# Attention beside a gated linear unit: K, Q and the output rows as dense tiles of 128 rows

## The chip, the cores and the metric

The kernel runs on one core of one Trainium2 chip. The metric is the device time of one execution in microseconds, the median of several runs. The core has a matrix engine (TensorE, PE in the profile; its weight loads are listed apart as PEld), a vector engine (VectorE, DVE), an engine for activation functions (ScalarE, ACT), a general engine (GpSimd, POOL), and SyncE (SP), which here only issues DMA transfers. Each runs its own list of instructions in order and waits on semaphores for the others. SBUF is the on-chip memory, of 128 partitions; PSUM holds matmul results in banks of 128 partitions by 512 numbers of 32 bits.

## What is computed

With x of 2048 rows and 640 columns, 32 heads of 20 columns, and a feed-forward width of 1728:

```python
xn = layernorm(x)                                # no scale, no shift
q, k, v = split(xn @ wqkv)                       # 32 heads of 20 columns each
p = softmax(q @ k.T / sqrt(20))                  # per head, 2048 x 2048
s = concat_heads(p @ v) @ wo
h = sigmoid(xn @ w_gate) * (xn @ w_up)
g = silu(h @ w_down)
out = x + s * g
```

Inputs and the output are bf16.

## The kernel before

**Tiles.** The work on attention is cut into passes: 4 chunks of 512 queries, and in each 8 groups of 4 heads, so 32 passes. A pass has 16 tiles of 128 keys for 4 heads, that is 64 score banks of 128 keys by 512 queries, and the whole program has 2048 of them. A head has only 20 columns, so the kernel lays each of the four heads of a group into a band of 32 partitions: `kT_all` holds K transposed, bands of 32 partitions by group by 2048 keys, and a tile `qT` holds the group's queries in the same bands. In a band the first row is an extra one: 1 in K and in Q a bound on the scores, which is subtracted inside the score matmul; rows 1 to 20 are the head; the others are zero. The bound of a query is a matmul of the absolute values of q with the maxima of |k| (`k_max` L121, `k_most` L118, `k_bound` L115, `q_abs` L127).

**One score bank.** A score matmul (L879) writes a bank of PSUM. Banks are taken in sets of 3 and of 2 in turn, and ACT takes the exponential of a whole set in one instruction (L901). Now and then one more bank, called spare, is scored and its exponential is made by four operations on DVE (L912, L917, L921, L925), when the planner finds DVE's backlog short. Then PV matmuls (L999) add eight banks at a time into one PSUM bank, `oacc`, in which each head has a band: a row of the sum of the exponentials and 20 rows of output.

**End of a pass.** `normalise` (L660 to L697) copies `oacc` to SBUF (`oev`, L667), sends the sums of the exponentials out to DRAM and back on POOL's DMAs, takes reciprocals, broadcasts them back over the bands (`rl`, four DMAs, L684) and multiplies (`oT`, L696).

**The other work** fills gaps between scores on PE as "jobs", generators that emit a few matmuls at a time and then hand an eviction to DVE or ACT: `k_job` (L470, K of one group and 512 keys), `v_job`, `q_job` (L493, Q of one pass), `gateup_job` (L524), `down_job` (L564), `out_job` (L604, eight matmuls per half of 320 columns, one for each group, with the output weights in bands, `wo_pad`), and `part_job` (L631), which for the last query chunk multiplies the six groups that are done early. Jobs share two PSUM banks (`take_bank`, `give_bank`), and at most two are under way.

**What sets the order.** No engine chooses its order at run time: a planner in the Python program keeps a clock for PE, models of ACT and DVE with the cells that their operations wait for, and a due score bank for every job. K's job for a group is due 40 banks before the pass that needs it, Q's 24. A cell (`Cell`) holds the time at which the planner believes a result is there; a transfer counts 3.4 us. When nothing else is ready and PE would be idle for long, `zero_add` (L979 to L986) issues a matmul of zeros into `oacc`. SP takes its DMAs strictly in the order in which they are emitted, and its DMAs use eight semaphores in turn, so that each one waits until the eighth before it has landed.

**Setup and tail.** A setup stage normalises x, transposes it, makes K for the first group and Q for the first pass; the weights of K and Q are copied to bands by POOL (`wkp`, `wqp`, `pad_copy` L206), those of the output by 32 DMAs (`load_wo`, L754). After the last score, PE finishes the last partial products (L646), DVE copies the last `oacc` (L1080), and the last two groups are projected (L1088).

Of the kernel before, what the change touches and what calls it, by code (L numbers as in the profile page):

```python
# [14 lines left out]
P = 128  # L15
# [6 lines left out]
V_CHUNKS = ((0, 16), (16, 32))  # L22
OBUFS, WB = 1, 2
# [16 lines left out]
def kernel(  # L40
# [46 lines left out]
    mk_all = const.tile([P, NG, 4], FP32, name="mk_all")  # L87
    mk = const.tile([P, NG], FP32, name="mk")
    bound = const.tile([P, NG, P], BF16, name="bound")
# [7 lines left out]
    wqp = persist.tile([P, KD, HEAD, 32], BF16, name="wqp")  # L97
    wo_pad = persist.tile([P, NG, D], BF16, name="wo_pad")
# [4 lines left out]
    wkp = ep.tile([P, KD, HEAD, 32], BF16, name="wkp")  # L103
    wv = ep.tile([P, KD, D], BF16, name="wv")

    def k_matmuls(ps, g, cols):
        for kd in range(KD):
            nc.tensor.matmul(ps, lhsT=wkp[:, kd, GH * g:GH * g + GH, :].rearrange("p h e -> p (h e)"),  # L108
                             rhs=xnT[:, kd, cols],
                             start=(kd == 0), stop=(kd == KD - 1))  # L110
            yield

    def k_bound(g):
        k_most(g)
        nc.vector.tensor_scalar(out=bound[:, g, :], in0=esum, scalar1=mk[:, g:g + 1], scalar2=None, op0=ALU.mult)  # L115

    def k_most(g):
        nc.vector.tensor_reduce(out=mk[:, g:g + 1], in_=mk_all[:, g, :], axis=AXISX, op=ALU.max)  # L118

    def k_max(src, g, c):  # L120
        nc.vector.tensor_reduce(out=mk_all[:, g, c:c + 1], in_=src, axis=AXISX, op=ALU.max,  # L121
                                apply_absolute_value=True)

    def q_abs(ps):
        absq = wk.tile([P, QC], BF16, tag="absq", bufs=1, name="absq")
        high = ps.bitcast(U16).rearrange("p (q two) -> p q two", two=2)[:, :, 1]
        nc.vector.tensor_scalar(out=absq.bitcast(U16), in0=high, scalar1=0x7FFF, scalar2=None,  # L127
                                op0=ALU.bitwise_and)
        return absq
# [11 lines left out]
    def q_matmuls(ps, cols, g):  # L141
        for kd in range(KD):
            nc.tensor.matmul(ps, lhsT=wqp[:, kd, GH * g:GH * g + GH, :].rearrange("p h e -> p (h e)"),  # L143
                             rhs=xnT[:, kd, cols],
                             start=(kd == 0), stop=(kd == KD - 1))
            yield

    V_SETUP = 4
    qTs = {}
    with tc.tile_pool(name="setup", bufs=1) as sp, \
            tc.tile_pool(name="ps0", bufs=1, space=bass.MemoryType.PSUM) as ps0:
        x_sb = sp.tile([P, TT, D], BF16, name="x_sb")
        wk_raw = sp.tile([P, KD, D], BF16, name="wk_raw")
        wq_raw = sp.tile([P, KD, D], BF16, name="wq_raw")
# [20 lines left out]
        load_w(wk_raw, 1)  # L178
        load_x(12, 4)
        load_w(wq_raw, 0)  # L180
# [7 lines left out]
        nc.vector.memset(wkp[:, :, GH:HEAD, 1 + Dh:32], 0.0)  # L188
        for w in (wkp, wqp):
            nc.gpsimd.memset(w[:, :, 0:GH, 0:1], 0.0)  # L190
            nc.gpsimd.memset(w[:, :, 0:GH, 1 + Dh:32], 0.0)
# [13 lines left out]
        def pad_copy(dst, raw, g0, g1):  # L205
            nc.gpsimd.tensor_copy(  # L206
                out=dst[:, :, GH * g0:GH * g1, 1:1 + Dh],
                in_=raw[:, :, GH * g0 * Dh:GH * g1 * Dh].rearrange("p k (h e) -> p k h e", e=Dh))
# [38 lines left out]
        def k_mm(c):  # L247
            kps[c] = ps0.tile([P, 512], FP32, tag="k", bufs=KBUFS, name="ps_k")
            for _ in k_matmuls(kps[c], 0, slice(c * 512, (c + 1) * 512)):
                pass  # L250
# [16 lines left out]
        def q_mm():  # L267
            first["ps"] = ps0.tile([P, 512], FP32, tag="q", bufs=1, name="ps_q")
            for _ in q_matmuls(first["ps"], slice(0, QC), 0):
                pass  # L270

        def q_bound():
            nc.tensor.matmul(first["ps"], lhsT=bound[:, 0, :], rhs=first["abs"], start=False, stop=True,
                             skip_group_check=True)

        def q_evict():
            qT = wk.tile([P, QC], BF16, tag="qT", bufs=2, name="qT")
# [20 lines left out]
        op(("wkp",), "POOL", 0.52, ["wk"], lambda: pad_copy(wkp, wk_raw, 0, 1))  # L298
        ends["wk"], ends["wq"], ends["wv"] = 10.8, 14.7, 16.7
        op(("wqp",), "POOL", 0.52, ["wq"], lambda: pad_copy(wqp, wq_raw, 0, 1))  # L300
        for c in range(4):
            op(("k", c), "PE", 1.3, [("xnT", 4 * c + i) for i in range(4)] + [("wkp",)]
               + ([("kmax", c - KBUFS), ("kadd", c - KBUFS)] if c >= KBUFS else []), lambda c=c: k_mm(c), 0.2)
            op(("kmax", c), "DVE", 0.64, [("k", c)], lambda c=c: k_max(kps[c], 0, c))
            op(("kadd", c), "ACT", 0.57, [("kmax", c)], lambda c=c: k_add(c), 0.6 * (c == 3))
        op(("kmost",), "DVE", 0.2, [("kmax", c) for c in range(4)], lambda: k_most(0))
        op(("kbound",), "ACT", 0.3, [("kmost",)],
           lambda: nc.scalar.activation(out=bound[:, 0, :], in_=esum, func=ACT.Identity, scale=mk[:, 0:1]))
# [30 lines left out]

        nc.gpsimd.memset(wkp[:, :, GH:HEAD, 0:1], 0.0)  # L340
        pad_copy(wkp, wk_raw, 1, 2)
        nc.gpsimd.memset(wqp[:, :, GH:HEAD, 0:1], 0.0)
        nc.gpsimd.memset(wqp[:, :, GH:HEAD, 1 + Dh:32], 0.0)
        pad_copy(wqp, wq_raw, 1, 2)
        pad_copy(wkp, wk_raw, 2, NG)
        pad_copy(wqp, wq_raw, 2, NG)
        nc.gpsimd.memset(v_all[:, :, HH:HEAD, 0:1], 1.0)
        nc.gpsimd.memset(wo_pad.rearrange("p g d -> p (g d)"), 0.0)
# [113 lines left out]
    kb_cells = {0: Cell(0.0)}  # L462
# [7 lines left out]
    def k_job(g, c):  # L470
        cols = slice(c * 512, (c + 1) * 512)
        held, ps = yield "bank",
        for _ in k_matmuls(ps, g, cols):
            yield "mm", MM5
        k_cells[g, c] = dve.add(630.0, [Cell(pe[0] + PE_OUT)], lambda: nc.vector.tensor_scalar(
            out=kT_all[:, g, cols], in0=ps, scalar1=e0[:, 0:1], scalar2=None, op0=ALU.add), 1)
        give_bank(held, k_cells[g, c])
        most = dve.add(620.0, [k_cells[g, c]], lambda: k_max(kT_all[:, g, cols], g, c), 2)
        kb_cells.setdefault((g, "max"), []).append(most)
# [672 lines left out]
```

## Time and profile before

| | |
|---|---|
| median of 3 runs | 915.73 us (915.34 to 917.61) |
| the profiled execution | 916.7 us, its span 914.8 us |
| PE busy | 805.1 us, 88% |
| DVE busy | 837.8 us, 92% |
| ACT busy | 880.2 us, 96% |
| POOL busy | 167.7 us, 18% |
| DMA traffic | 49.5 MB, 54 GB/s over the span |

The first exponential of the main stage starts at 32.4 us and the last one ends at 896.6 us, so that a score bank takes 0.42 us on average.

A profile line of a group reads: line of the program, engine, operation, the tile written and the tiles read, shape and type, count; then the busy time in total and the mean of one in ns; then how long the engine stood idle in front of these instructions, and which instruction on which engine ended the wait. Times of neighbouring instructions overlap, so the distance from one start to the next can be shorter than the mean. A line by window gives its length, the busy time of PE, PEld, DVE, ACT and POOL with the number of instructions, the granted clock of PE (1.00 is full), the share of the DMA engines' time, and GB/s.

### The profile page before, as it was taken

How to read it: one execution, taken by the hardware profiler on the slowest of the kernel's cores; microseconds unless marked ns; L12 is line 12 of the kernel's file. 1: busy time of each engine (PE TensorE's matmuls, PEld its weight loads, DVE VectorE, ACT ScalarE, POOL GpSimd, SP SyncE). 2: the span in 40 equal slices, each digit the busy share in tenths (PEclk: the TensorE clock that was granted, in tenths of full speed). 3: DMA queues.
4: the chain of work that ended last, by engine and by line, in shares of the span. 5: the costliest groups of instructions: out<-in, count | busy, mean ns of one | idle time of the engine just before them, and what ended most of it. 6: DMA issues, size and time to landing. Idle time of an engine off the chain costs nothing.

```text
span 914.8 us, 16028 instructions
## 1 busy us (share of the span) xinstructions
PE 805.1 (88%) x6027; PEld 274.3 (30%) x6027; DVE 837.8 (92%) x1424; ACT 880.2 (96%) x845; POOL 167.7 (18%) x307
## 2 busy tenths in 40 slices
PE   5898889988888998898889998998899999989995
PEld 2332223322222233322223333222233322223333
DVE  8799999998999999999999999999889967989995
ACT  6989999999999999999999999999999999999992
POOL 7601111011111111211111112111011221011121
PEclk9999999999999999999999999999999999999997
DMA  6070000002222112322221132322102333220003
GB/s 223 22 227 14 13 14 14 2 14 56 49 64 46 32 59 70 51 56 56 57 49 28 52 100 35 66 62 57 38 20 85 79 49 71 45 56 21 13 17 84
DMA packets 91901, 49.50 MB, mean 54 GB/s; under 512 B 78548, under 2 KB 86132, under 8 KB 91696
## 3 DMA queue, kind: packets, MB, share of 16 engines
q1 hardware_dynamic: 81616, 32.37, 14.0%
q0 software_dynamic: 10208, 16.11, 7.8%
q8 instruction: 47, 0.77, 0.3%
q14 instruction: 30, 0.25, 0.1%
HBM read 40.74 MB, written 9.03 MB: 54 GB/s over the span
## 4 chain that ended last, share of the span: by engine, by line
ACT 64%; issue 16%; DVE 10%; PE 8%; DMA 1%; POOL 0%; SPq 0%; DVEq 0%; ACTq 0%; POOLq 0%
ACT p L901 59%; ACT tnh L548 3%; PE sc L879 3%; DVE dy L912 2%; DVE du L917 1%; DVE du L921 1%; PE work L541 1%; DVE p L925 1%; PE oacc L999 1%; DVE stats L214 1%; PE work L133 1%; PE work L554 1%; ACT td L587 1%; DMA x_sb<-in_A_x_dram 0%; PE work L143 0%
## 5 line engine op out<-in xcount | busy, mean ns | idle before, releaser
L901 ACT ACTIVATE p<-sc 128x1536 bf16<-128x1536 f32 x725 | 840.5, 1399 | 6.6 <-PE oacc L999 5.2
L879 PE MATMUL sc<-qT,kT_all 32*128 32x512 bf16 x1813 | 283.1, 382 | 76.7 <-ACT p L901 70.4
L879 PEld LDWEIGHTS <-kT_all 32*128 32x128 bf16 x2048 | 90.9, 90 | 320.0 <-issue 310.3
L912 DVE TENSOR_SCALAR dy<-spare 128x512 f32<-128x512 f32 x235 | 160.8, 684 | 26.0 <-PE spare L879 23.9
L917 DVE SCALAR_TENSOR_TENSOR du<-dy 128x512 f32<-128x512 uint16 x235 | 161.3, 686 | 4.6
L925 DVE SCALAR_TENSOR_TENSOR p<-du,dy 128x512 uint16<-128x512 f32 x235 | 161.0, 685 | 4.0
L921 DVE SCALAR_TENSOR_TENSOR du<-du,dy 128x512 f32<-128x512 f32 x235 | 161.1, 685 | 3.5
L999 PE MATMUL oacc<-p,v_all 128*21 128x512 bf16 x2048 | 157.4, 383 | 0.0
L668 POOL DMA_DIRECT2D den_dram<-oev x31 | 18.0, 582 | 397.1 <-DVE oev L667 387.8
L879 PE MATMUL spare<-qT,kT_all 32*128 32x512 bf16 x235 | 90.1, 383 | 0.0
L576 PE MATMUL work<-wd,hT 128*128 128x320 bf16 x448 | 85.4, 302 | 0.3 <-DVE dy L912 0.2
L541 PE MATMUL work<-xnT,wg 128*128 128x512 bf16 (+1 forms) x280 | 81.2, 383 | 1.0 <-DVE dy L912 0.3
L554 PE MATMUL work<-xnT,wu 128*128 128x512 bf16 (+1 forms) x280 | 76.7, 381 | 1.8 <-DVE dy L912 0.9
L684 POOL DMA_DIRECT2D rl<-rec_dram x124 | 62.1, 513 | 55.0 <-DMA rec_dram<-den 46.4
L576 PEld LDWEIGHTS <-hT 128*128 128x128 bf16 x448 | 35.7, 97 | 46.9 <-issue 35.3
L999 PEld LDWEIGHTS <-v_all 128*21 128x21 bf16 x2048 | 29.7, 90 | 63.3 <-issue 62.3
L143 PE MATMUL work<-xnT,wqp 128*128 128x512 bf16 x155 | 43.9, 382 | 2.5 <-DVE dy L912 2.0
L548 ACT ACTIVATE tnh<-work 128x512 bf16<-128x512 f32 (+1 forms) x56 | 44.3, 791 | 0.0
L558 DVE SCALAR_TENSOR_TENSOR hT<-tnh,work 128x512 bf16<-128x512 bf16 (+1 forms) x56 | 38.0, 679 | 5.4 <-ACT tnh L548 3.9
L678 POOL DMA_DIRECT2D rec_dram<-den x31 | 17.0, 550 | 132.2 <-DVE den L677 132.2
L108 PE MATMUL work<-xnT,wkp 128*128 128x512 bf16 x140 | 39.8, 383 | 0.9 <-DVE dy L912 0.9
L614 PE MATMUL work<-wo_pad,oT 128*128 128x320 bf16 x192 | 36.1, 302 | 0.7 <-DVE dy L912 0.7
(106 smaller groups left out, 556.1 us busy)
## 6 DMA issues: line engine op xcount, KB each, us to landing
wg<-in_B_w_gate_dram SPq DMA_DIRECT2D x52, 160.0 KB
wu<-in_B_w_up_dram SPq DMA_DIRECT2D x52, 160.0 KB
rl<-rec_dram POOLq DMA_DIRECT2D x124, 64.0 KB, 2.3
gq_dram<-d POOLq DMA_DIRECT2D x12, 320.0 KB, 2.5
gqr<-gq_dram SPq DMA_DIRECT2D x12, 320.0 KB
wd<-in_B_w_down_dram SPq DMA_DIRECT2D x1, 2080.0 KB
out_dram<-in_A_x_dram SPq DMA_DIRECT2D x1, 1920.0 KB
out_dram<-gqr POOLq DMA_DIRECT2D x12, 160.0 KB, 3.7
```

The source lines that it names most:

```text
L541: nc.tensor.matmul(psg[0:fsz, :], lhsT=wg[:, kd, 0:fsz], rhs=xnT[:, kd, cols], start=(kd == 0), stop=(kd == KD - 1))
L548: nc.scalar.activation(out=made["t"][0:fsz, :], in_=psg[0:fsz, :], func=ACT.Tanh, scale=0.5)
L554: nc.tensor.matmul(psu[0:fsz, :], lhsT=wu[:, kd, 0:fsz], rhs=xnT[:, kd, cols], start=(kd == 0), stop=(kd == KD - 1))
L576: nc.tensor.matmul(psd[:, 0:HALF], lhsT=hT[0:fsz, kf, t4 * P:(t4 + 1) * P], rhs=glu[1][0:fsz, kf, e0_:e1_], start=(kf == 0), stop=(kf == N ...
L684: nc.gpsimd.dma_start(out=t["rl"][32 * j:32 * j + 32, :], in_=rec_dram[n, j:j + 1, :].to_broadcast([32, QC]))
L879: nc.tensor.matmul(ps, lhsT=kT_all[32 * j:32 * j + 32, g, kt * P:(kt + 1) * P], rhs=qTs[qc, g][32 * j:32 * j + 32, :], start=True, stop=Tr ...
L901: nc.scalar.activation(out=buf.tile(), in_=ps, func=ACT.Exp, bias=EXP_BIAS, scale=exp_scale)
L912: nc.vector.tensor_scalar(out=t["y"], in0=ps, scalar1=LEAST, scalar2=None, op0=ALU.max)
L917: nc.vector.scalar_tensor_tensor(out=t["u"], in0=t["f"], scalar=CUBE_2, in1=t["f"], op0=ALU.add, op1=ALU.mult)
L921: nc.vector.scalar_tensor_tensor(out=t["u"], in0=t["u"], scalar=CUBE_1, in1=t["f"], op0=ALU.add, op1=ALU.mult)
L925: nc.vector.scalar_tensor_tensor(out=buf.tile()[:, 0, :].bitcast(U16), in0=t["u"], scalar=CUBE_SCALE, in1=t["y"], op0=ALU.mult, op1=ALU.add)
L999: nc.tensor.matmul(oacc[32 * j:32 * j + 1 + Dh, :], lhsT=v_all[:, b % PER_PASS // GH, GH * g + j, 0:1 + Dh], rhs=buf.ap[:, i, :], start=(n ...
```

## The change

K and Q are no longer projected group by group into bands of 32, of which 20 rows are used, but as five dense tiles of 128 rows (`DENSE`), out of weights in their plain layout (`wkd`, `wqd`, 640 columns and the first group's 80 once more at the end). The rows are then sent to their bands by DMA.

- K: a job makes one tile for 512 keys. DVE copies the PSUM bank to a tile `kd` (two buffers), and 7 or 8 DMAs on SP carry each head's rows to `kT_all`. The maxima are taken from `kd`. The constant row of every band is copied by 7 DMAs ahead of the main stage. The first group is made in bands as before.
- Q: a job makes one dense tile (`qd`, one buffer for all five). The bounds of all heads are accumulated by a separate `bound_job` out of the absolute values of `qd`, and DVE evicts them as a tile of 32 rows. `pads()` sends the rows to `qT` (three buffers) by 4 or 5 DMAs for q and one for the bounds, up to two passes ahead.
- Scores read 21 rows of a band and not 32.
- Output: at the end of a pass 4 or 5 DMAs on SP carry the rows of `oT` into a dense tile `od`; `out_job` needs five matmuls per half in place of eight and `part_job` four in place of six. The output weights come by one DMA (`wo_all`), and by eight in bands for the last two groups (`wo_end`).
- Due times: K 60 banks ahead in place of 40, Q's tiles 50, the bounds 36. `gqr` has two buffers in place of four; the last chunk's gate is kept in `kT_all`.

The core of the diff:

```diff
+    def dense_matmuls(ps, w, t, cols):
+        for kd in range(KD):
+            nc.tensor.matmul(ps, lhsT=w[:, kd, ROWS + P * t:ROWS + P * (t + 1)], rhs=xnT[:, kd, cols],
                              start=(kd == 0), stop=(kd == KD - 1))
             yield
...
-        wk_raw = sp.tile([P, KD, D], BF16, name="wk_raw")
-        wq_raw = sp.tile([P, KD, D], BF16, name="wq_raw")
+        wkp = sp.tile([P, KD, GH, 32], BF16, name="wkp")
+        wqp = sp.tile([P, KD, GH, 32], BF16, name="wqp")
...
-        nc.gpsimd.memset(wo_pad.rearrange("p g d -> p (g d)"), 0.0)
+        nc.gpsimd.memset(wo_end, 0.0)
...
-    def k_job(g, c):
+    def k_job(t, c):
...
-        k_cells[g, c] = dve.add(630.0, [Cell(pe[0] + PE_OUT)], lambda: nc.vector.tensor_scalar(
-            out=kT_all[:, g, cols], in0=ps, scalar1=e0[:, 0:1], scalar2=None, op0=ALU.add), 1)
-        give_bank(held, k_cells[g, c])
...
+        def evict():
+            made["k"] = ep.tile([P, 512], BF16, tag="kd", bufs=2, name="kd")
+            nc.vector.tensor_copy(out=made["k"], in_=ps)
+            for h, r, d, n in pieces(t):
+                g, j = divmod(h, GH)
+                if g:
+                    nc.sync.dma_start(out=kT_all[32 * j + 1 + d:32 * j + 1 + d + n, g, cols], in_=made["k"][r:r + n, :])
+            landed[t, c] = dve.t + DMA_WAIT
...
+        done = dve.add(606.0, [Cell(pe[0] + PE_OUT), *kd_free[-2:-1]], evict, 1)
+        give_bank(held, done)
+        kd_free.append(dve.add(606.0, [done], lambda: k_max(made["k"], t, c), 2))
...
+        qd_cells[qc, t] = dve.add(606.0, [Cell(pe[0] + PE_OUT)], lambda: nc.vector.tensor_scalar(
+            out=qd[:, t, :], in0=ps, scalar1=q_scale, scalar2=None, op0=ALU.mult), 1)
...
+            def absolute(t):
+                def fn():
+                    made[t] = wk.tile([P, QC], BF16, tag="absq", bufs=2, name="absq")
+                    nc.vector.tensor_scalar(out=made[t].bitcast(U16), in0=qd[:, t, :].bitcast(U16), scalar1=0x7FFF,
+                                            scalar2=None, op0=ALU.bitwise_and)
+                return dve.add(200.0, [], fn, 0)
...
+                nc.tensor.matmul(ps, lhsT=bounds[:, t, :], rhs=made[t], start=(k == 0), stop=(k == len(tiles) - 1))
...
+                row = wk.tile([HEAD, QC], BF16, tag="row", bufs=2, name="row")
+                nc.vector.tensor_scalar(out=row, in0=ps[0:HEAD, :], scalar1=ONE, scalar2=None, op0=ALU.add)
...
+    def pads():
+        n = next_pad[0]
+        if n == NQC * NG or at_bank[0] < PER_PASS * (n - 2):
+            return False
...
+        qT = wk.tile([P, QC], BF16, tag="qT", bufs=3, name="qT")
+        for t in TILES[g]:
+            for h, r, d, k in pieces(t):
+                if h // GH == g:
+                    at_row = 32 * (h % GH) + 1 + d
+                    nc.sync.dma_start(out=qT[at_row:at_row + k, :], in_=qd[r:r + k, t, :])
+        row = (g - 1) % NG * GH
+        nc.sync.dma_start(out=qT[0:P:32, :], in_=b_tiles[qc, g][row:row + GH, :])
...
-            for g in range(NG):
-                nc.tensor.matmul(pss[:, 0:HALF], lhsT=oTs[qc, g][:, t4 * P:(t4 + 1) * P],
-                                 rhs=wo_pad[:, g, h * HALF:(h + 1) * HALF], start=(g == 0), stop=(g == NG - 1))
+            for k in range(KD):
+                nc.tensor.matmul(pss[:, 0:HALF], lhsT=ods[qc][:, k, t4 * P:(t4 + 1) * P],
+                                 rhs=wo_all[:, k, h * HALF:(h + 1) * HALF], start=(k == 0), stop=(k == KD - 1))
...
-            oTs[qc, g] = wk.tile([P, QC], BF16, tag="oT", bufs=NG + 4, name="oT")
+            oT = oTs[qc, g] = wk.tile([P, QC], BF16, tag="oT", bufs=3, name="oT")
...
+                    nc.sync.dma_start(out=ods[qc][a % P:a % P + b - a, a // P, :], in_=oT[at_row:at_row + b - a, :])
...
-    K_DUE, Q_DUE, V_DUE, OUT_DUE = -40, -24, 6, 4 * PER_PASS
+    K_DUE, Q_DUE, B_DUE, V_DUE, OUT_DUE = -60, -50, -36, 6, 4 * PER_PASS
...
     def load_wo():
-        for h in range(HEAD):
+        nc.sync.dma_start(out=wo_all, in_=A_wo.rearrange("(k p) d -> p k d", p=P))
+        for h in range(HEAD - 2 * GH, HEAD):
...
-        nc.tensor.matmul(ps, lhsT=kT_all[32 * j:32 * j + 32, g, kt * P:(kt + 1) * P],
-                         rhs=qTs[qc, g][32 * j:32 * j + 32, :], start=True, stop=True,
+        nc.tensor.matmul(ps, lhsT=kT_all[32 * j:32 * j + 1 + Dh, g, kt * P:(kt + 1) * P],
+                         rhs=qTs[qc, g][32 * j:32 * j + 1 + Dh, :], start=True, stop=True,
                          tile_position=(32 * j, 0))
...
+    for g in range(1, NG):
+        nc.sync.dma_start(out=kT_all[0:P:32, g, :], in_=kT_all[0:P:32, 0, :])
     load_wo()
```

In the lines of the changed program that the prediction names, L486 is the copy to `kd`, L565 that of the row of bounds, and L797 the DMAs of `oT`'s rows into `od`.

## The prediction, made before the changed kernel was run

> **What bounds the kernel now.** Read first: the share of each engine over the span, and the chain that ended last.
>
> ```profile
> PE 805.1 (88%) x6027; PEld 274.3 (30%) x6027; DVE 837.8 (92%) x1424; ACT 880.2 (96%) x845; POOL 167.7 (18%) x307
> ACT 64%; issue 16%; DVE 10%; PE 8%; DMA 1%; POOL 0%; SPq 0%; DVEq 0%; ACTq 0%; POOLq 0%
> ```
>
> ScalarE (ACT) is the bound and nearly all of its time is the exponential, L901; VectorE (DVE) stands close behind. The groups by form say what ACT does and how little it waits:
>
> ```profile
> L901 ACT ACTIVATE p<-sc 128x1536 bf16<-128x1536 f32 x363 | 585.1, 1612 | 3.7 <-PE oacc L999 2.5 <-POOL wqp L206 1.2
> L901 ACT ACTIVATE p<-sc 128x1024 bf16<-128x1024 f32 x362 | 428.9, 1185 | 3.0 <-PE oacc L999 2.6 <-PE sc L879 0.2
> L879 PE MATMUL sc<-qT,kT_all 32*128 32x512 bf16 x1813 | 283.1, 382 | 76.7 <-ACT p L901 70.4
> L108 PE MATMUL work<-xnT,wkp 128*128 128x512 bf16 x140 | 39.8, 383 | 0.9 <-DVE dy L912 0.9
> L143 PE MATMUL work<-xnT,wqp 128*128 128x512 bf16 x155 | 43.9, 382 | 2.5 <-DVE dy L912 2.0 <-DVE mk L118 0.2
> L614 PE MATMUL work<-wo_pad,oT 128*128 128x320 bf16 x192 | 36.1, 302 | 0.7 <-DVE dy L912 0.7
> L475 DVE TENSOR_SCALAR kT_all<-work,e 128x512 bf16<-128x512 f32 x28 | 20.8, 742 | 0.0
> L506 DVE TENSOR_SCALAR qT<-work,e_one 128x512 bf16<-128x512 f32 x31 | 23.1, 744 | 1.7 <-PE work L501 1.6
> L127 DVE TENSOR_SCALAR absq<-work 128x512 uint16<-128x512 uint16 x31 | 21.0, 677 | 0.1
> L984 PE MATMUL oacc<-xnT,zero 128*128 128x512 bf16 x59 | 21.4, 388 | 0.0
> ```
>
> The scores wait 70.4 us for the exponentials, not the other way round. Neighbours overlap, so I use start to start: 1.331 us for an exponential of three banks, 0.904 of two; on DVE about 0.60 (512 columns) and 0.66 (L475, L506); on PE 0.216 and 0.136 (512 and 320 columns). The table by stage shows where ACT is not full:
>
> ```profile
> 40.00:70.00 30.00, 26.76 (x203) 9.94 (x202) 29.51 (x54) 25.62 (x23) 0.38 (x1) 1.00 0.60 186
> 70.00:100.00 30.00, 25.71 (x195) 7.39 (x191) 29.70 (x52) 30.00 (x28) 5.13 (x10) 1.00 0.04 11
> 100.00:160.00 60.00, 53.22 (x405) 17.62 (x405) 58.75 (x104) 60.00 (x54) 9.41 (x19) 1.00 0.06 15
> 700.00:800.00 100.00, 92.15 (x687) 29.66 (x680) 81.48 (x134) 100.00 (x95) 17.47 (x30) 1.00 0.28 61
> 900.00:915.00 15.00, 5.59 (x32) 3.63 (x32) 8.02 (x16) 0.00 (x0) 0.51 (x1) 0.65 0.25 72
> ```
>
> Columns: window, length, busy time of PE, PEld, DVE, ACT, POOL, granted clock, DMA share, GB/s. From 70 us to the tail ACT is full; at 40 to 70 it lacks 4.4 us while DVE has 0.5 us left of 30. Added up start to start, ACT loses 5.6 us by 90 and 16.9 in all, the rest thinly spread. So time saved on PE is not time saved; what can move the end is ACT's own work, the tail, and DVE or a transfer being late before 160 us. Last, SP's order of work and the chain's end:
>
> ```profile
> 37.71 11.90 SPq L754 DMA_DIRECT2D wo_pad<-in_A_wo_dram  x32
> 894.42 0.40 PE sc L879 x3
> 894.82 1.74 PE work L646 x12
> 896.55 0.54 PE oacc L999 x8
> 897.10 1.75 PE work L646 x12
> ```
>
> SP issues a DMA every 0.37 us in order; these of 20x640 land 1.63 us after issue. Twelve partial output products stand at the end behind the last exponential.
>
> **The change part by part.** Sums go against the profiled execution's own 916.7 us (span 914.8); that lies 1.0 above the median of 915.7, and I carry the difference over.
>
> *PE.* K goes from 140 matmuls to 100, Q from 155 to 100, bounds from 31 to 24: 102 x 0.216 = 22.0 us. Output and parts go from 240 to 152: 88 x 0.136 = 12.0 us. The order of after holds 142 zero matmuls for 59 (83 x 0.216 = 17.9 us back), and PE waits for ACT anyway. Worth nothing; if PE were the bound it would be 16 us.
>
> *ACT.* By the order of after, 361 and 360 exponentials for 363 and 362: ten banks go to DVE. 2 x 1.331 + 2 x 0.904 = -4.5 us on the bound.
>
> *DVE.* Ten banks more, four operations each (+40 x 0.60 = +24 us); K's evictions 28 to 20 (-5.3), its maxima 28 to 20 (-4.8), Q's 31 evictions to 20 dense and 8 of rows (-3.7), absolute values 31 to 24 (-4.2; these read SBUF now, so the row of 677 ns from PSUM is an upper bound, and half of it a lower one). Net about +6 us or less, mostly late, where 700 to 800 shows 18.5 us free. Off the path there.
>
> *Tail.* In after the partial products are in front of the last score. Before, the last exponential ends at 896.63 and the last oev copy at 899.97: 3.34 us. Without L646 between them I keep a PV batch 0.54 and the copy 0.61: about 1.2. So -2.1 us (0 to -2.3).
>
> *DMAs on SP: 175 become 593.* New are 136 for K, 140 + 31 for Q's rows, 135 for the output rows, 7 for K's constant row; the weights of the output fall from 32 to 9. No row of before has an SBUF to SBUF DMA. Nearest are the 20x640 loads (1.63) and rl on POOL (2.3); I take 1.65 and 0.37 of issue, with 2.3 as the upper end and 1.3 as the lower. In a steady pass Q's rows go out about 50 us ahead and the output rows are needed a chunk later: 9 x 0.37 = 3.3 us of SP in 27 us, covered. POOL loses its 4.7 us memset; it is off the path.
>
> *The start, where it is not covered.* The scores begin at 32.4 as before, a bank per 0.422 us.
> 1. The third K eviction reuses a buffer that the first one's seven DMAs read. SP first issues 7 constant rows, wo and 8 pieces; a rotation of eight semaphores makes these wait for wo (800 KB, about 4 us). First K piece about 38.1, last landed 42.0, DVE there at 40.8: DVE 1.2 us late, ACT up to 1. Before lost 2.1 near 50 us, and I count this inside the next step.
> 2. Pass 2 begins with bank 129, ideally at 86.4. Its q needs the row of bounds (L565). DVE comes to the first oev at about 69.1 (68.6 before); 33 instructions stand between, 30 of them full: 18.3 us, so the row ends at 87.4. On SP the four pieces of the output rows (L797) come first, waiting for oT 0.6 later; then six of q: 87.4 + 0.6 + 9 x 0.375 + 1.65 + 0.05 = 93.1, first exponential 93.6. Lost by then 7.2 us. Behind this score every PE instruction waits, so DVE's spare banks starve too.
> 3. At bank 134 a K matmul job stands in front of the scores; its PSUM bank is freed by the eviction of K tile 2's third chunk, whose buffer is freed by eight DMAs behind the five of the next pass's q: about 4.9 us after step 2. ACT is idle some 4.6 us again, less the few banks between.
> Together 11.8 us where before lost 5.6: +6.2. With 1.3 us per landing it is +5, with 2.3 and slower issue (0.45) +9.
> PE stands still 3.1 and 4.9 us there. At 900 to 915, with PE busy 5.6 of 15, the granted clock is 0.65; everywhere else 1.00. If the ten us behind each gap ran at 0.65, a full PE would lose 3.5 us each; lower bound 0. I take 1.5 in all: ACT's pace leaves PE a tenth free, and one of the gaps is short. +1.5 us.
> [...]
>
> *From the second chunk on.* All heads' bounds are one chain of five matmuls with absolute values between, at banks near 384, 896, 1408; PE follows DVE there (0 to 1 us each). gqr has two buffers for four and its load stands behind q pieces: DVE up to 2.5 us late three times, ACT 0 to 1 each. Together +2.0 (0 to +5).
>
> Sum: -4.5 - 2.1 + 6.2 + 1.5 + 2.0 = +3.1: profile 919.8, median 918.8.
>
> [...]
>
> **The rivals.**
> A. The start is covered: q of pass 2 lands before bank 129. It needs the row on DVE by about 80.7, not 87.4, and then steps 2 and 3 vanish together. For it: DVE's absolute values from SBUF and the earlier due points save 2 or 3 us, and before itself had DVE 99% full here and lost only 0.3 us at 70 to 160. Against: 33 instructions at 0.60 can't shrink by 6.7. -4.5 - 2.1 with 2.0 in the middle or less: 909 to 912. Faster; it decides when the landing is under 88.
> B. It cancels: only one of steps 2 and 3 shows and the clock stays: -6.6 + 2.0 + 4 or so, 914 to 917.
> C. SP becomes the bound: output rows wait on SP for DVE and hold the gate weights and q behind them, in every pass. For it: one queue, in order, eight semaphores. Against: 3.3 us of issue in a pass of 27. At 1 us in 30 passes: 930 to 945.
> D. The clock falls behind each gap for long: PE, 88% busy, then trails for 10 us twice at 0.65: +7 where I have +1.5, 922 to 926. For it the 900 to 915 row; against, 1.00 in every stage before it. [...]
> E. The change doesn't do what it says, in that PE's saving shows nowhere: that is my own reading already, so PE's busy time should fall by 16 us at most and the span by none of it.
>
> **How the numbers follow.** Forecast (a stall at pass 2 that outweighs the gain), 917 to 923: 0.37. D: 0.10. C: 0.06. B: 0.20. A: 0.27. The prediction is 918.8. Change under 0.3% (2.75 us) can't be told from none. Faster is below 913.0: A, less a little, 0.27. Within: B and the edge of the forecast, 0.25. Slower above 918.5: 0.48. The range for 8 in 10 runs from 909 to 927: out are C, the far end of D and A's lower edge (landing at once and no loss at 40 to 70, 906). The forecast's own range is 916 to 923.
>
> **What would show it.** Right: ACT idle about 7 us before the first score of pass 2 (near 87 to 94), released by a DMA into qT; a second gap of 4 to 5 us right after, behind L486 on DVE waiting for DMAs; ACT's sum of exponentials 4.5 us less; 142 zero matmuls; no L646 in the last chain. Wrong: ACT full from 70 to 110; an SBUF to SBUF landing well off 1.65; idle ACT once per pass; L565 ending well before 87.

## The result and the profile after

The changed kernel takes 986.49 us (median of 4 runs, 976.5 to 994.0) against 915.54 (915.23 to 917.61) before: 1.073 times the time, 95% interval 1.065 to 1.081. The longest of the four is a slow execution, and the ratio is that of the means without it, 983.2 and 916.0. The prediction was 918.8, its range 909 to 927. The profiled execution has a span of 984.3 us against 914.8.

Shares of the engines and the chain that ended last, of the changed kernel:

```profile
PE 846.4 (86%) x5920; PEld 271.3 (28%) x5920; DVE 837.7 (85%) x1433; ACT 882.2 (90%) x841; POOL 158.9 (16%) x306
ACT 39%; PE 20%; issue 16%; DVE 14%; SPq 6%; DMA 5%; POOL 1%; DVEq 0%; ACTq 0%; POOLq 0%
```

ACT has the same work and a longer span; of the chain it holds 39% and not 64%, and SP's queue and the DMAs, 1% before, have 11%. PE has 107 instructions fewer and is busy 41 us longer, and the mean granted clock is 0.924 where it was 0.994. The groups by form:

```profile
L1014 ACT ACTIVATE p<-sc 128x1536 bf16<-128x1536 f32 x361 | 568.4, 1575 | 26.7 <-PE sc L992 19.0 <-PE spare L992 5.6 <-issue 1.2
L1014 ACT ACTIVATE p<-sc 128x1024 bf16<-128x1024 f32 x360 | 412.9, 1147 | 49.9 <-PE sc L992 26.4 <-PE spare L992 17.1 <-PE oacc L1112 5.8
L1097 PE MATMUL oacc<-xnT,zero 128*128 128x512 bf16 x142 | 50.0, 406 | 0.0
L119 PE MATMUL work<-xnT,wkd 128*128 128x512 bf16 x100 | 32.1, 433 | 10.4 <-DVE kd L486 10.1 <-DVE v_all L152 0.3
L486 DVE CAST kd<-work 128x512 bf16<-128x512 f32 x20 | 13.7, 686 | 29.3 <-DMA kT_all<-kd 26.7 <-PE work L119 2.5
L551 DVE TENSOR_SCALAR absq<-qd 128x512 uint16<-128x512 uint16 x24 | 6.2, 284 | 1.9 <-PE work L558 1.8
```

ACT stands idle for 76.6 us in front of exponentials where it did for 6.7; 68.1 of that is ended by a score of PE (`sc` or `spare`). Behind that stands K's copy, L486: DVE waits 26.7 us for DMAs that still read its buffer. Added up start to start with the durations of the prediction, ACT loses 92.1 us where it lost 16.9: +75.2, less 4.5 of its own work and 2.1 at the end, plus 0.9 behind the last copy of oacc, is +69.5, the whole difference of the spans. Where it lies: 49.2 us before 170 us (7.6 before the change), 42.9 after (9.4 before).

**The start.** By stage:

```profile
40.00:70.00 30.00, 21.73 (x116) 6.57 (x115) 16.98 (x32) 15.25 (x14) 0.00 (x0) 0.72 0.10 22
70.00:100.00 30.00, 25.46 (x185) 8.19 (x181) 26.97 (x48) 25.67 (x23) 3.84 (x7) 0.95 0.10 24
100.00:130.00 30.00, 16.00 (x76) 3.81 (x73) 12.08 (x23) 9.20 (x9) 0.58 (x1) 0.65 0.10 22
130.00:170.00 40.00, 36.60 (x231) 10.08 (x230) 33.17 (x62) 34.39 (x31) 4.79 (x9) 0.79 0.14 33
```

At 100 to 130 ACT works 9.2 of 30 us; the granted clock is 0.65. The DMA engines are at 10%: not bandwidth, but the line in front of them. SP's own time line from 80 to 130 us:

```profile
83.66 21.28 SPq L490 DMA_DIRECT2D kT_all<-kd  x28
105.04 2.98 SPq L797 DMA_DIRECT2D od<-oT  x4
108.07 3.67 SPq L591 DMA_DIRECT2D qT<-qd  x5
111.79 0.55 SPq L593 DMA_DIRECT2D qT<-row  x1
112.45 2.99 SPq L591 DMA_DIRECT2D qT<-qd  x4
115.48 0.56 SPq L593 DMA_DIRECT2D qT<-row  x1
116.14 14.07 SPq L490 DMA_DIRECT2D kT_all<-kd  x19
```

SP issues without a pause: 28 K pieces in 21.3 us, 0.75 each, then the output's rows, then q. The 32 loads of the prediction's fence took 0.37 each. DVE, the lines with the long waits for K's buffers, from the first K tile on, and those that the chain passes; then PE:

```profile
46.87 0.69 DVE L486 CAST kd<-work 128x512 bf16<-128x512 f32 x1 [5.93 <-DMA kT_all<-kd]
52.25 0.69 DVE L486 CAST kd<-work 128x512 bf16<-128x512 f32 x1 [2.89 <-DMA kT_all<-kd]
96.29 0.69 DVE L486 CAST kd<-work 128x512 bf16<-128x512 f32 x1 [2.72 <-DMA kT_all<-kd]
103.73 0.68 DVE L565 TENSOR_SCALAR row<-work 32x512 bf16<-32x512 f32 x1 [1.11 <-PE work L558]
104.34 0.67 DVE L786 TENSOR_TENSOR oT<-oev,rl 128x512 bf16<-128x512 f32 x1
123.45 0.69 DVE L486 CAST kd<-work 128x512 bf16<-128x512 f32 x1 [13.91 <-DMA kT_all<-kd]
```

```profile
113.52 0.40 PE L992 MATMUL sc<-qT,kT_all 21*128 21x512 bf16 x4 [3.91 <-DMA qT<-row]
124.20 2.29 PE L119 MATMUL work<-xnT,wkd 128*128 128x512 bf16 x5 [10.09 <-DVE kd L486]
```

The row of bounds ends at 104.4, the last DMA into qT is issued at 111.8 and lands 1.69 later, and the first score of pass 2 runs at 113.5. Then DVE stands 13.9 us for a kd buffer, PE behind it, and bank 134 comes at 126.4. In the chain of work from 84 to 130 us, SP's issues of K pieces alone hold 49%.

**The rest.** From 300 us to the tail the granted clock falls to 0.50 seven times, for 3.4 to 20.5 us, 78.5 us in all (the expectations below speak of nine and of eight; eight is the count with the tail's); before it fell only in the tail. Four windows around one fall; they are cut at multiples of 3.413 us from a change of the clock, since all changes in this trace lie such multiples apart:

```profile
465.85:469.26 3.41, 3.37 (x24) 1.15 (x23) 3.27 (x7) 3.41 (x4) 0.55 (x1) 1.00 0.23 50
469.26:472.67 3.41, 2.38 (x20) 0.83 (x19) 3.31 (x7) 3.41 (x5) 1.98 (x4) 1.00 0.42 125
472.67:476.09 3.42, 3.42 (x15) 0.72 (x12) 3.32 (x6) 2.93 (x4) 0.00 (x0) 0.50 0.03 5
476.09:479.50 3.41, 3.41 (x17) 0.46 (x15) 1.97 (x3) 2.33 (x3) 0.00 (x0) 0.50 0.22 48
```

In the second line PE is busy 2.38 of 3.41 us, in pieces with gaps of at most 0.6 us, and ACT is full: the bound does not wait, and yet the next window is at half clock. Then PE is full and ACT no longer is. PE is now the bound, with the same work: matmuls of 512 columns in a row start 0.426 us apart at 0.50, and 0.216 at 1.00.

The tail of the changed kernel, in the chain:

```profile
963.47 1.72 ACT p L1014
965.24 0.39 PE sc L992 x3
965.63 0.54 PE oacc L1112 x8
966.17 0.97 PE oacc L1097 x4
967.14 0.77 PE oacc L1112 x8
967.93 0.70 DVE oev L1196
```

No partial products stand there any more. The last exponential ends at 967.44 and the copy at 968.62: 1.18 us for 3.33 before, as predicted.

### The profile page after: what moved, and what is told of

Same layout as the page of the kernel before. It is cut to its first block, busy times and chain, and to the rows that moved or that the text cites. A ratio compares the mean times of both kernels' runs of the same rounds, so it can differ in the third digit from the quotient of the medians.

```text
span 984.3 us, 16453 instructions
## 1 busy us (share of the span) xinstructions
PE 846.4 (86%) x5920; PEld 271.3 (28%) x5920; DVE 837.7 (85%) x1433; ACT 882.2 (90%) x841; POOL 158.9 (16%) x306
## 4 chain that ended last, share of the span: by engine, by line
ACT 39%; PE 20%; issue 16%; DVE 14%; SPq 6%; DMA 5%; POOL 1%; DVEq 0%; ACTq 0%; POOLq 0%
ACT p L1014 36%; PE sc L992 6%; SPq L490 3%; PE oacc L1112 3%; PE work L628 3%; DVE dy L1025 3%; DVE du L1030 2%; DVE du L1034 2%; DVE p L1038 2%; PE work L641 2%; ACT tnh L635 2%; SPq L591 1%; PE work L702 1%; PE work L119 1%; PE work L147 1%
## 5 line engine op out<-in xcount | busy, mean ns | idle before, releaser
L1014 ACT ACTIVATE p<-sc 128x1536 bf16<-128x1536 f32 x721 | 838.8, 1361 | 76.6 <-PE sc L992 45.5
L992 PE MATMUL sc<-qT,kT_all 21*128 21x512 bf16 x1803 | 294.6, 400 | 78.4 <-ACT p L1014 68.7
L1025 DVE TENSOR_SCALAR dy<-spare 128x512 f32<-128x512 f32 x245 | 167.9, 685 | 47.4 <-PE spare L992 44.6
L992 PEld LDWEIGHTS <-kT_all 21*128 21x128 bf16 x2048 | 92.8, 91 | 349.2 <-issue 334.8
L1030 DVE SCALAR_TENSOR_TENSOR du<-dy 128x512 f32<-128x512 uint16 x245 | 168.3, 687 | 5.1
L1112 PE MATMUL oacc<-p,v_all 128*21 128x512 bf16 x2048 | 169.2, 405 | 3.7 <-DVE p L1038 3.5
L1038 DVE SCALAR_TENSOR_TENSOR p<-du,dy 128x512 uint16<-128x512 f32 x245 | 167.9, 685 | 4.8
L992 PE MATMUL spare<-qT,kT_all 21*128 21x512 bf16 x245 | 98.3, 401 | 4.1 <-DVE kd L486 2.2
L1097 PE MATMUL oacc<-xnT,zero 128*128 128x512 bf16 x142 | 50.0, 406 | 0.0
L645 DVE SCALAR_TENSOR_TENSOR hT<-tnh,work 128x512 bf16<-128x512 bf16 (+1 forms) x56 | 37.9, 677 | 12.9 <-PE work L641 12.3
L119 PE MATMUL work<-xnT,wkd 128*128 128x512 bf16 x100 | 32.1, 433 | 10.4 <-DVE kd L486 10.1
L635 ACT ACTIVATE tnh<-work 128x512 bf16<-128x512 f32 (+1 forms) x56 | 40.6, 725 | 0.0
L486 DVE CAST kd<-work 128x512 bf16<-128x512 f32 x20 | 13.7, 686 | 29.3 <-DMA kT_all<-kd 26.7
```

The lines of the kernel that those rows point to most:

```text
L635: nc.scalar.activation(out=made["t"][0:fsz, :], in_=psg[0:fsz, :], func=ACT.Tanh, scale=0.5)
L992: nc.tensor.matmul(ps, lhsT=kT_all[32 * j:32 * j + 1 + Dh, g, kt * P:(kt + 1) * P], rhs=qTs[qc, g][32 * j:32 * j + 1 + Dh, :], start=True, ...
L1014: nc.scalar.activation(out=buf.tile(), in_=ps, func=ACT.Exp, bias=EXP_BIAS, scale=exp_scale)
L1025: nc.vector.tensor_scalar(out=t["y"], in0=ps, scalar1=LEAST, scalar2=None, op0=ALU.max)
L1030: nc.vector.scalar_tensor_tensor(out=t["u"], in0=t["f"], scalar=CUBE_2, in1=t["f"], op0=ALU.add, op1=ALU.mult)
L1038: nc.vector.scalar_tensor_tensor(out=buf.tile()[:, 0, :].bitcast(U16), in0=t["u"], scalar=CUBE_SCALE, in1=t["y"], op0=ALU.mult, op1=ALU.add)
```

## The experiments

Times are medians, "before" is the kernel before on the same chip. The last columns are of the profiled execution: ACT's losses before and after 170 us, and the time at half clock between 170 us and the tail.

| run | us | before, us | lost before 170 | lost after | half clock |
|---|---|---|---|---|---|
| before | 915.5 | | 7.6 | 9.4 | 0 |
| changed | 986.5 | 915.5 | 49.2 | 42.9 | 78.5 |
| e1, before with 21 rows | 918.0 | 916.0 | 8.9 | 13.0 | 10.2 |
| e2, more zero matmuls | 974.8 | 916.0 | 46.8 | 35.2 | 61.5 |
| e3, K's rows on POOL | 960.5 | 916.0 | 24.3 | 43.9 | 85.4 |
| e4, output part alone | 926.7 | 916.0 | 8.1 | 22.6 | 20.4 |
| e5, the same on POOL | 914.5 | 916.4 | 8.1 | 10.5 | 3.4 |
| e6, two queues | 932.6 | 916.4 | 11.2 | 28.1 | 44.3 |
| e7, scores of 32 rows | 958.1 | 916.4 | 41.3 | 24.4 | 17.0 |
| e8, four gqr buffers | 982.6 | 916.4 | 49.7 | 39.2 | 68.3 |
| e9, e6 and e7 together | 921.7 | 916.5 | 14.2 | 12.3 | 3.4 |
| e10, e9 and q on POOL | 932.4 | 916.5 | 19.1 | 20.0 | 17.0 |
| e11, eight kd buffers | 982.8 | 916.5 | 33.9 | 35.4 | 58.0 |

**e1: the kernel before, with scores of 21 rows.**

```diff
-        nc.tensor.matmul(ps, lhsT=kT_all[32 * j:32 * j + 32, g, kt * P:(kt + 1) * P],
-                         rhs=qTs[qc, g][32 * j:32 * j + 32, :], start=True, stop=True,
+        nc.tensor.matmul(ps, lhsT=kT_all[32 * j:32 * j + 1 + Dh, g, kt * P:(kt + 1) * P],
+                         rhs=qTs[qc, g][32 * j:32 * j + 1 + Dh, :], start=True, stop=True,
```

> The kernel before, with the score matmuls reading 21 rows of a band and not 32; nothing else changed. In the changed kernel the granted clock fell to 0.50 nine more times after 300 us, in windows where PE had no long idle time. Theory R (the array's activity counts rows, and the shorter scores starve it): the clock falls here too, at least three times in the main loop, and the time is 925 to 950 us. Theory S (the changed order leaves stretches of 3.4 us with PE streaming less than half of the time; the 21 rows are innocent): the clock stays at 1.00 up to the tail and the time is that of before, 914 to 918 us.

In the profile the clock fell three times in the main loop (at 120, 421 and 820 us); that execution took 921.3 us, the longest of ten. Over all ten the mean granted clock is 0.991, over the thirteen of before 0.995, and the time is 1.0018 times that of before (1.0004 to 1.0033). The instruction streams are the same but for the rows, so the lower clock (0.991 for 0.995) goes with the rows alone. In the order of before it costs some 2 us where theory R had 9 or more: its falls, not its price.

**e2: the changed kernel with more zero matmuls.**

```diff
-    WINDOW, ENOUGH = 3400.0, 2300.0
+    WINDOW, ENOUGH = 3400.0, 2900.0
```

> The changed kernel, with the planner's limit for zero matmuls raised from 2300 to 2900 ns of streaming in every 3400 (ENOUGH). Theory S: with more zero matmuls no stretch after 170 us falls under half, the clock stays at 1.00 there, and of the some 37 us that ACT lost after 170 us about 30 come back: 950 to 962 us; the losses before 170 us (49 us) stay. Theory M (ACT's late losses are from DVE and SP being late, and the clock only follows): the clock stays up but the time falls by less than 10 us. If PE becomes the bound by the zeros, slower than 986.

A miss for both. 316 zero matmuls in place of 142 took 12 us off. After 600 us ACT loses 4.4 in place of 26.4, but between 300 and 600 it loses 23.3 in place of 14.2, with falls of 20.5 and 23.9 us. At a clock of 0.50 a zero matmul costs PE 0.426 us in place of 0.216, as above; that this is why these falls last longer was not tested.

**e3: K's rows issued by POOL.**

```diff
-                    nc.sync.dma_start(out=kT_all[32 * j + 1 + d:32 * j + 1 + d + n, g, cols], in_=made["k"][r:r + n, :])
+                    nc.gpsimd.dma_start(out=kT_all[32 * j + 1 + d:32 * j + 1 + d + n, g, cols], in_=made["k"][r:r + n, :])
```

> The changed kernel, with the DMAs of K's rows (136 of 20x512) issued by POOL and not by SP; Q's and the output's stay on SP. Theory I (an issue from SBUF to SBUF occupies SP for 0.75 us and that spacing, not the landing of 1.9 us, makes the gaps between 40 and 130 us): POOL's DMAs show 0.50 to 0.58 us of issue, K's seven pieces need 4 us and not 5.3, and they are no longer in line with Q's and the output's: ACT's losses before 170 us fall from 49 to 25 to 35 us, 960 to 975 us. Theory L (the landing decides): within 5 us of 986.

The group of these DMAs, by form:

```profile
L490 POOL DMA_DIRECT2D kT_all<-kd x128 | 65.0, 517 | 20.1 <-DVE kd L486 13.6 <-issue 2.6 <-DVE absq L551 2.5
```

0.52 us each, and the start's losses are halved: 960.5 us. The pieces are the same; the line that they stand in has changed, and with it the price of an issue (0.52 for 0.71). Theory I; this run does not part the two.

**e4: the output part alone, on the kernel before; e5: the same with its DMAs on POOL.** Of e4 the core, and e5's one line:

```diff
+    wo_all = persist.tile([P, KD, D], BF16, name="wo_all")
+    wo_end = persist.tile([P, 2, D], BF16, name="wo_end")
...
+            for k in range(KD):
+                nc.tensor.matmul(pss[:, 0:HALF], lhsT=ods[qc][:, k, t4 * P:(t4 + 1) * P],
...
+                    nc.sync.dma_start(out=ods[qc][a % P:a % P + b - a, a // P, :], in_=oT[at_row:at_row + b - a, :])
```

```diff
-                    nc.sync.dma_start(out=ods[qc][a % P:a % P + b - a, a // P, :], in_=oT[at_row:at_row + b - a, :])
+                    nc.gpsimd.dma_start(out=ods[qc][a % P:a % P + b - a, a // P, :], in_=oT[at_row:at_row + b - a, :])
```

> The kernel before with the output part of the change alone: rows of oT by DMA to the dense tile, five and four matmuls for eight and six, one load of the output weights and eight in bands; K and Q as before. Theory E (the loss is K's and Q's pieces at the start): no gap between 90 and 130 us, time 910 to 916 us; the 23 loads fewer at the start and the shorter tail may show as 2 to 4 us. Theory C (DMAs of the output rows wait on SP for DVE and hold the gate weights behind them): 925 us or more, with PE waiting for wg.

> As the run of the output alone, but the DMAs of oT's rows are issued by POOL and not by SP. There they had held SP until DVE made oT, so that the load of wd and the copy into out (4 MB together) went out at 200 us in place of 50 and met the softmax sums' DMA, which took 6.3 us and not 2. Theory Q (that line on SP is the loss): the burst goes out near 50 us again, nothing is lost at 205 to 220, and the time falls from 926.7 to 913 to 919 us. Theory P (the loss is from the output order itself): it stays at 922 to 928.

e4 is 10.7 us slower than before (1.011, 1.008 to 1.014), e5 faster (0.9977, 0.9967 to 0.9986). The windows from 200 to 220 us, e4 first:

```profile
205.00:210.00 5.00, 4.06 (x29) 1.12 (x28) 2.53 (x4) 5.00 (x5) 0.57 (x1) 1.00 1.10 400
210.00:215.00 5.00, 0.64 (x3) 0.09 (x2) 2.20 (x6) 1.60 (x2) 0.56 (x1) 0.75 0.86 298
215.00:220.00 5.00, 4.84 (x24) 0.94 (x27) 3.52 (x7) 2.68 (x3) 1.99 (x4) 0.50 0.18 54
```

And e5:

```profile
205.00:210.00 5.00, 4.06 (x32) 1.03 (x28) 4.93 (x11) 5.00 (x5) 0.84 (x2) 1.00 0.01 2
210.00:215.00 5.00, 4.59 (x37) 1.46 (x36) 4.45 (x8) 5.00 (x6) 1.70 (x4) 1.00 0.30 85
215.00:220.00 5.00, 4.22 (x30) 1.57 (x29) 4.90 (x9) 5.00 (x6) 0.00 (x0) 1.00 0.20 45
```

In e4 the DMA engines are full at 400 GB/s: wd and the copy into out, 4 MB, leave SP at 200 us because the output's rows stand in front of them and wait for DVE. DVE waits 5.2 us for the softmax sums from DRAM (`den`, a transfer of 8 KB), PE has nothing to do (busy 0.64 of 5 us), and the clock falls to 0.50. In e5 SP runs ahead of the program again, the burst leaves at 38 us, and nothing is lost. Theory C's time came without its sign, since PE waits nowhere for wg in e4. It is theory Q, and the prediction's rival C in a form that it did not have: not a wait in every pass, but one large transfer moved to where another is waited for. e5 is the one version here that beats the kernel before, by 0.2%; its gains are 2.0 us in the tail (1.30 for 3.33) and some 1.7 of ACT's work (one exponential of three banks and one of two fewer, one of a single bank more), less 1.6 more lost.

**e6: two queues.**

```diff
-                    nc.sync.dma_start(out=kT_all[32 * j + 1 + d:32 * j + 1 + d + n, g, cols], in_=made["k"][r:r + n, :])
+                    (nc.sync if j % 2 else nc.gpsimd).dma_start(out=kT_all[32 * j + 1 + d:32 * j + 1 + d + n, g, cols], in_=made["k"][r:r + n, :])
...
-            made["k"] = ep.tile([P, 512], BF16, tag="kd", bufs=2, name="kd")
+            made["k"] = ep.tile([P, 512], BF16, tag="kd", bufs=8, name="kd")
...
-                    nc.sync.dma_start(out=ods[qc][a % P:a % P + b - a, a // P, :], in_=oT[at_row:at_row + b - a, :])
+                    nc.gpsimd.dma_start(out=ods[qc][a % P:a % P + b - a, a // P, :], in_=oT[at_row:at_row + b - a, :])
```

> The changed kernel, with K's rows issued by SP and POOL in turn (by band), the output's rows by POOL, and eight kd buffers in place of two. Theory I: a K chunk needs 3.5 issues of 0.75 and not 7, and DVE no longer waits for the landing of the chunk before the last: ACT's losses before 170 us fall from 49 to 10 to 20 us, and the time to 945 to 958, the losses after 300 us (41) being as they are. Theory L (something other than these DMAs at the start): over 30 us lost before 170, time above 965.

```profile
40.00:70.00 30.00, 26.72 (x199) 10.34 (x198) 28.19 (x53) 25.05 (x23) 4.88 (x10) 1.00 0.10 23
70.00:100.00 30.00, 27.25 (x194) 7.97 (x192) 29.79 (x55) 27.33 (x25) 22.67 (x45) 1.00 0.21 49
100.00:130.00 30.00, 26.70 (x195) 8.53 (x194) 28.27 (x53) 29.02 (x26) 12.77 (x25) 0.94 0.19 43
```

These stages, the same as shown of the changed kernel, are nearly full: 11.2 us lost before 170 in place of 49.2. The time fell further than expected, to 932.6, as the late losses shrank too.

**e7: scores of 32 rows in the changed kernel; e9: e6 and e7 together.** For both the scores are as before; the unused rows are set to zero, and K's constant rows are issued by POOL and not by SP.

```diff
-        nc.tensor.matmul(ps, lhsT=kT_all[32 * j:32 * j + 1 + Dh, g, kt * P:(kt + 1) * P],
-                         rhs=qTs[qc, g][32 * j:32 * j + 1 + Dh, :], start=True, stop=True,
+        nc.tensor.matmul(ps, lhsT=kT_all[32 * j:32 * j + 32, g, kt * P:(kt + 1) * P],
+                         rhs=qTs[qc, g][32 * j:32 * j + 32, :], start=True, stop=True,
...
+            nc.gpsimd.memset(kT_all[:, g, :], 0.0)
```

> The changed kernel, with the scores reading all 32 rows of a band as before; for it K's bands and three q tiles are set to zero by POOL, and POOL issues K's constant rows, which shifts the first 60 us. Theory R (the meter behind the clock counts rows; a fit over six runs gives a microsecond of 21-row scores half the weight of one of 32 rows): after 300 us the eight intervals at half clock become at most three, and ACT's losses there fall from 41 us to under 20: 955 to 968 us. Theory S (the order alone leaves PE idle): five or more intervals, 978 to 990 us.

> The run with two queues and the one with scores of 32 rows put together: K's rows by SP and POOL in turn, the output's rows by POOL, eight kd buffers, scores of 32 rows (K's bands set to zero by POOL, two groups ahead of the main stage and five after the first K tile). Theory R plus I (two separate causes, queue at the start and rows of the array later): ACT's losses before 170 us stay near 11 and those after 300 us fall from 27 to 8 to 14: 914 to 922 us. If the memsets hold POOL's pieces at the start, up to 930. Theory S (order): after 300 us still over 20 lost, 928 or more.

e7 takes 28 us off the changed kernel. The start is little better (41.3 for 49.2), and since K's constant rows have moved too, those 8 us can't be put down to the array's rows. The rest is late: four falls after 300 us in place of seven, of 17.0 us together in place of 78.5, and ACT's losses there are 21.4 us in place of 40.6. I had expected at most three falls and under 20 us: just missed, but much nearer to R than to S, and 958.1 lies in R's range. In e9, with the queues mended as well, there is one fall after 170 us, of 3.4, and the time is 921.7, 1.006 times before (1.0045 to 1.008). The clock by fortieths of the span in e9:

```profile
PEclk9999999999999999999999999999999999999998
```

and in the changed kernel:

```profile
PEclk9979669999999999999699999987999779899997
```

So 54 of the 71 us go with the three edits of e6 to the line of DMAs, and another 11 with e9's. By ACT's losses after 170 us the rows take 18.5 us off the changed kernel (42.9 to 24.4) and 15.8 off e6 (28.1 to 12.3), nearly the same; the 28 and the 11 differ by what the same edits do at the start, 8 us less lost in e7 and 3 more in e9.

**e8: four gqr buffers.**

```diff
-        gqr = glu[0].tile([P, D], FP32, tag="gqr", bufs=2, name="gqr")
+        gqr = glu[0].tile([P, D], FP32, tag="gqr", bufs=4, name="gqr")
```

> The changed kernel with four gqr buffers, as before the change, in place of two. At 371 to 378 us a gqr load stood behind the landing of the output's accumulating DMA (3.7 us) and DVE waited 3.85 us for it, ACT lost 5. Theory G: these waits of DVE for gqr (6.7 us in all) go, ACT's losses fall by 5 to 8 us, 976 to 982. If q's rows on SP hold the load instead: DVE still waits 4 us or more, 983 to 989.

```profile
DVE gqr L708 <- DMA gqr<-gq_dram: 6.8, 3, 4.0
```

The wait is as it was (6.7 us, longest 3.8, in the changed kernel). The buffers are not the cause of it: on SP the load stands behind five output and six q DMAs of about 0.75 us, from 366.8 to 375.3 in the changed kernel and from 367.5 to 376.4 here, and is issued at their end.

**e10: q's rows on POOL too.**

```diff
-                    nc.sync.dma_start(out=qT[at_row:at_row + k, :], in_=qd[r:r + k, t, :])
+                    nc.gpsimd.dma_start(out=qT[at_row:at_row + k, :], in_=qd[r:r + k, t, :])
...
-        nc.sync.dma_start(out=qT[0:P:32, :], in_=b_tiles[qc, g][row:row + GH, :])
+        nc.gpsimd.dma_start(out=qT[0:P:32, :], in_=b_tiles[qc, g][row:row + GH, :])
```

> As the run with two queues and 32 rows, and q's rows by POOL too, so that SP has only half of K's pieces and the loads. Theory G (gqr's load stands on SP behind q's and the output's rows): DVE no longer waits for gqr (4.8 to 6.8 us before), 2 to 4 us less than the run beside it. Against: POOL must issue q's rows between the softmax sums' DMAs, for which it waits some 6 us in every pass, so that q comes later at pass 2 and the time is 3 to 10 us more.

DVE's waits for gqr are gone, as theory G has it, but the time is 10.7 us above e9's. 4.9 of it are at the start, where q comes later, and 6.8 at 190 to 210 us, where, as in e4, the softmax sums took long: 6.35 and 4.74 us out and back. The cause is e4's too: behind K's pieces, wd and the copy into out leave SP at 180.3 to 182.6 us, and the DMA engines are full when the sums go by:

```profile
190.00:195.00 5.00, 3.50 (x25) 0.99 (x26) 1.68 (x3) 5.00 (x6) 0.57 (x1) 1.00 1.03 303
```

The burst is late in e6 and e9 as well, from 179.0 and 182.0 us, without such a loss.

**e11: eight kd buffers alone.**

```diff
-            made["k"] = ep.tile([P, 512], BF16, tag="kd", bufs=2, name="kd")
+            made["k"] = ep.tile([P, 512], BF16, tag="kd", bufs=8, name="kd")
```

> The changed kernel with eight kd buffers in place of two and nothing else: SP still issues all rows. Theory B (DVE's wait for a buffer is what starves the scores): ACT's losses before 170 us fall from 49 to under 25, 955 to 965 us. Theory I (the spacing of 0.75 us on SP is it; q's rows of pass 2 and K's of group 2 still arrive when SP gets to them): the first gap, at 42 to 56 us, falls by 5 to 8 us, those from 95 to 126 stay over 15: 970 to 982 us.

Four executions gave 963.2 (the profiled one), 982.7, 982.8 and 984.3, so no interval is given; the table has the median of the four beside the losses of the profiled one, and whether the buffers alone gain any time stays open. In the profile DVE no longer waits for kd at all, and still 33.9 us are lost before 170, 16.6 of them between 90 and 120. SP shows why, from 80 us on:

```profile
79.78 21.29 SPq L490 DMA_DIRECT2D kT_all<-kd  x28
101.17 2.98 SPq L797 DMA_DIRECT2D od<-oT  x4
104.20 3.67 SPq L591 DMA_DIRECT2D qT<-qd  x5
107.92 0.55 SPq L593 DMA_DIRECT2D qT<-row  x1
```

The same line, 4 us earlier. The buffers are worth about a third of the start's loss in this execution; q of pass 2 waits for SP, not for DVE.

## Why the prediction was wrong

- **The bound and PE's saving: right.** 107 instructions fewer on PE brought nothing; 142 zero matmuls came as the order had them. PE's busy time rose by 41 us where I had it fall: ahead of the tail the clock stood at 0.50 for 136.5 us. DVE's busy time came out at 837.7 for 837.8, where I had up to 6 more.
- **ACT's work, -4.5 us, and the tail, -2.1: right.** 361 and 360 exponentials; 1.18 us in place of 3.33 at the end.
- **"Nearest are the 20x640 loads (1.63) ... I take 1.65 and 0.37 of issue": the step that failed.** One of 20x512 between parts of SBUF occupies SP for 0.71 us, 0.75 with the gap, and lands after 1.9. I had an upper end for issue of 0.45. The landing was 15% off and would have cost little; the issue was off by two and is paid 7 times per K chunk, 28 times per tile. (K's rows are 128 DMAs and not the 136 that I wrote; my 593 fits 128.)
- **Steps 1 to 3: right in place and order, wrong in size.** Step 1: DVE 1.2 us late by my sum, 5.9 and then 2.9 measured, and the clock at 0.50 from 46.0 to 63.1. Step 2: from the row's end to the first score of pass 2 I had 5.7 us; it took 9.1, nine DMAs at 0.75. But the row itself ended at 104.4 and not at 87.4. At twice the price step 1 was no single stall: the first copy of oacc began at 81.8, where I had 69.1, and the second K tile then waited for SP again. In e6, where the line is relieved, these stages are nearly full. Step 3: 4.9 us predicted, 12.9 measured from bank 129 to 134. Together ACT lost 42.1 us up to the end of step 3 for my 11.8, and 7.1 more by 170. The transfer of wo that step 1 counts at about 4 us landed 4.8 after its issue. The signs that I had named came: ACT idle 8.2 us before pass 2's first score, from 105.8 to 114.0, and 10.8 us behind L486.
- **Rival C (SP becomes the bound), at 0.06: at the start SP was the bound, though not by C's mechanism.** C had the output's rows waiting for DVE, 1 us in every pass; what filled SP were K's pieces, by their price. My reason against it, 3.3 us of issue in a pass of 27, held for steady passes only and used the wrong price; at the start K's 28 pieces alone take 21 us of SP in a pass. I had worked out SP's occupation for the pass where it is lowest.
- **Rival D (the clock), at 0.10, and my +1.5: too small.** I let the clock fall only behind two gaps, and at 0.65; that was the mean of a window, and the clock itself is 1.00 or 0.50 in the traces of before and of the changed kernel. It fell seven more times after 300 us. I read the shorter scores as free, since ACT sets the pace. They were not free for the clock: with 32 rows in place of 21 its time at 0.50 after 170 us fell from 78.5 us to 17.0 (e7) and from 44.3 to 3.4 (e9 for e6), and 21 rows in the order of before took its mean from 0.995 to 0.991 (e1). No term of the sum had the 21 rows at all: this is the second step that failed, and the losses after 170 us rose by 33.5 us, of which e7 and e9 put 16 to 19 down to the rows.
- **"From the second chunk on", +2.0: the wait was right** (gqr behind q's pieces on SP, up to 2.5 us; measured 3.8), and with it came a fall of the clock, which I had not priced.
- **Bounds from SBUF:** 284 ns per absolute value, below my lower bound of half of 677; off the path.

What stays open: why the rows cost some 2 us in the order of before (e1) and 16 to 19 us of late losses in the new one (e7, e9). The new order has fewer dense matmuls and more stalls on SP's line; no run here parts these two.

## What to carry to other kernels

Price a DMA's issue from a row with the same source and target (on SP here 0.33 us from DRAM, 0.71 between parts of SBUF), and count the line of its queue in the stage where most DMAs stand in it, not on average. A queue that only loaded ran far ahead of the program here (in e5 wd left SP at 38 us); DMAs in it that waited for a computation ended that, and moved the transfers behind them to a worse place (in e4 wd left at 200 us, ahead of a softmax sum that DVE then waited 5.2 us for). On a kernel whose clock falls as easily as here (16 to 19 us of late losses went with the rows), count what a change takes from the array (rows, and perhaps dense matmuls), even where the array has time to spare.

## What the runs showed of the hardware

- **Issue on SP differed with the kind of transfer.** From DRAM to SBUF, 20x640: 0.33 us (the 32 loads of `wo_pad` before). Between parts of SBUF, the time that all 128 K pieces took, from the view of the tile, min, median and max in ns:

```profile
L490 SPq DMA_DIRECT2D kT_all<-kd x128: 554/707/913, 40.3 to 213.4; - x128
```

  Pieces of 16 rows took 0.55, of 8 rows 0.65, of 20 rows 0.71 and of 12 rows 0.73: not in the order of their bytes. Issued by POOL the same pieces took 0.52 (e3).
- **The clock fell without idleness.** In the traces of before and of the changed kernel the granted clock is 1.00 or 0.50, and its changes lie multiples of 3.413 us apart. Ahead of the fall shown above PE was busy 2.38 of 3.41 us, with no gap over 0.6.
- **A sum that marks the falls.** I took all windows at full clock from 16 us on of six profiles (before, changed, e1 to e4), 41 ahead of a fall and 1456 others, and summed by kind the time in which matmuls streamed. One weighted sum, an estimate fitted to these windows, parts the falls from the others with about 5 errors: with 1.27 for a microsecond of dense matmul of 128 rows, 0.55 for a score of 32 rows, 0.27 for a score of 21 rows and 0.27 for a PV matmul, windows ahead of a fall lie below 1.7 and the others above. In before and the changed kernel that holds for all 13 falls and all but at most one of 486 others. On e5 to e8, which had no part in the fit, the same sum marks 29 to 31 of 32 falls, and 6 or 7 of the other 964 windows wrongly. (The ends of matmuls are modelled in the profile, so it depends on where in its record a matmul is taken to stream.) The fit does not show that rows count: with one weight for both kinds of score (dense 1, scores 0.2, PV 0.25, limit 1.33) it makes 3 to 8 errors, about as few. No run shows what the hardware counts. That the clock fell more with fewer rows rests on e1, e7 and e9, with the figures above, and that 21 rows count half of 32 is not shown.
